# Weight conversion spread differently: one 64-bit chunk per attention turn instead of two, its scaling on GpSimd, and a new written order of a turn

## The chip, the cores and the metric

The kernel runs on 1 core of one Trainium2 chip. The metric is the device time of one execution in microseconds. "Before" was timed three times; the median is 724.79 us.

## The reference, cut to what matters

```python
def reference(**kw):                      # B=4, H=8, S=576, D=64, d_model=512, hidden 2048
    # attention with a learned relative bias
    scores = q @ k^T / 8 + bias(relu(x @ w1 + b1) @ w2)   # bias is [H, S, S], the same for all B
    attn = softmax(scores)                                # + 1e-9 in the divisor
    x = (attn @ v) as [B, S, 512]
    # Fourier mixing and a two-layer network
    u  = x + Re(fft(fft(x, axis=1), axis=2))
    un = (u - mean(u)) / sqrt(var(u) + 1e-6)
    return u + relu(un @ w_ch1) @ w_ch2
```

`w_ch1` (512 x 2048) and `w_ch2` (2048 x 512) arrive as 64-bit floats. Nothing on the chip multiplies 64-bit floats, so the kernel takes the two 32-bit words of each number and puts a 32-bit float together from them.

## The kernel before

**Stages.** First the bias of all eight heads is computed (up to about 62 us). Then come 16 units of attention, a unit being one pair of heads of one batch element. Unit n is worked on in "turn" n; a turn lasts about 13.6 us. After the last unit a tail mixes the first batch element, and from about 300 us the dense network runs: batch 0 alone (up to about 390 us), batch 1, batches 2 and 3 as a pair, and the 64 left-over rows of each.

**The turn.** `turn_of` (line 598) walks through a list of tokens, `ORDER`; TensorE, VectorE and ScalarE execute their shares in exactly that order, and so does SyncE, which issues the loads and stores. GpSimd's order is left to the compiler's scheduler. A quote after a token means "of the unit before", two quotes "two units before". The tokens are:

- `S0` to `S8`: TensorE computes one of nine score blocks into PSUM (line 276). Pool `sps` has two banks, so a block must wait for the `D` of the block two before it.
- `D0` to `D8`: VectorE adds the bias, writes the result to SBUF and takes the row maximum (line 297).
- `X0` to `X8`: ScalarE's exponential with row sums (line 312).
- `R'`, `P0'` to `P4'`: TensorE transposes the probabilities of the unit before into PSUM (line 444). `E''` transposes the finished output of the unit before that. They and the output `o` of the value product share two PSUM buffers (`place`), taken in turn, so that each waits until the one two before it has been read out.
- `VR0'`, `VR1'`, `V0'` to `V4'`: ScalarE copies a transposed tile to SBUF (line 434). With a small `v`, VectorE does it (line 436). In the order before, that one is tile 3.
- `A0'` to `A4'`: TensorE's value product, 40 matmuls (line 525). `O'`: ScalarE reads it out (line 536).
- `Q0'`, `Q1'`, `Y1''`, `Y2''`: the division by the row sum, on ScalarE and VectorE. Two tiny copies across the partition halves (line 550) go by DMA.
- `W0` to `W3` and `U0` to `U3`: the conversion (`widen`, line 154) of one chunk of `w_ch1` (`W`) and one of `w_ch2` (`U`), 128 x 512 numbers each: step 0 scales the upper word as a float on ScalarE (line 162), steps 1 to 3 are bit operations on VectorE (lines 167, 168, 169). After step 3 the chunk is stored as 32-bit floats in HBM and the next raw chunk is fetched.

In between, `prep` splits the next unit's q and k into a high and a low part on GpSimd (lines 215 and 219).

**Where the chunks go.** There are 16 of each weight. The turns listed in `WIDE`, twelve of the fifteen, convert one of each, so 24 of 32 are done in the attention. The turns 4 and 8 (and 1) convert none. The last turn (15) is written out in `TAIL`, which goes on with the mixing of batch 0. The other 8 are converted in dense batch 0 by `widen_rest`, there with all four steps on VectorE and with the raw loads issued by ScalarE. The list of these pieces is merged by weights with the layers and with the mixing of batch 1 (`run`); VectorE keeps the resulting order, the other engines' order is the scheduler's.

**A dense layer** (`layer`, `down`): ScalarE and GpSimd split the two weights into high and low parts (lines 1009, 1010), TensorE does 12 matmuls up (line 1044), ScalarE and VectorE make the two parts of the relu (`hh`, `hl`, lines 1052, 1053), TensorE does 12 matmuls down (line 1069), one layer later.

Of the kernel before, what the change touches and what calls it, by code (L numbers as in the profile page):

```python
# [20 lines left out]
P = 128  # L21
# [12 lines left out]
WIDE = [2, 3, 5, 6, 7, 9, 10, 11, 12, 13, 14, 15]  # L34
NEED = [0, 1, 3, 2]
KAT, QAT = 14, 36
# [13 lines left out]
S1 R' S2 VR0' X4' E'' D1 D2 Y1'' S0 VR1' Q0' D0 S4 Y2'' X1 P0' X2 S3 D4 V0' D3 P1' S6 Q1' D6 S7 V1' P2' V2' P3'  # L50
W0 D7 v3' X6 S5 S8 P4' D8 A0' D5 X0 V4' W1 A1' U0 A2' X8 X3 X5 W2 W3 U1 U2 A3' U3 X7 A4' O'
# [3 lines left out]
S1 S7' D1 D7' X7' S2 D2 P0' S4 V0' D4 P1' S8' S3 V1' D8' X8' X1 D3 P2' S6 V2' Q0' D6 P3' S0 R' Q1' D0 S7 V3'  # L55
VR0' vR1' P4' X0 D7 S8 V4' D8 S5 X2 D5 X3 A0' A1' A2' X8 X6 A3' X5 X7 A4' O'
# [74 lines left out]
def body(ctx, tc, a, out):  # L131
# [22 lines left out]
    def widen(src, dst, raw, q=nc.sync, on_act=True):  # L154
# [26 lines left out]
    vp = pool("vp", 3, stack=late, side="right")  # L181
# [238 lines left out]
    with ExitStack() as st:  # L420
# [99 lines left out]
        def value(u, j):  # L520
# [21 lines left out]
        def recip(u):  # L542
# [20 lines left out]
        def scaled(u, w):  # L563
# [22 lines left out]
            "Q": lambda u, w: (recip if w == "Q1" else add_tiny)(u),  # L586
# [11 lines left out]
        def turn_of(n, between):  # L598

            for i, w in enumerate(SECOND if n == 1 else ORDER):  # L600
                w, u = w.rstrip("'"), n - w.count("'")
                if w[0] in "WU":
                    if n in WIDE:
# [12 lines left out]
        orders = st.enter_context(ExitStack())  # L616
        wide, uf = {}, {}
# [4 lines left out]
        def fetch(which, n):  # L622

            if which == "W":
                f = rawp.tile([P, 512], F32, tag="wf", name="wf")
                t = widen(a["m1"][:, P * n:P * n + P].rearrange("(k p) c -> p k c", p=P), f, raw_tile(rawp))
                t.append(lambda: nc.sync.dma_start(w1_d[n].rearrange("p k c -> p (k c)"), f))
            else:
                f = rawu.tile([P, DM], F32, tag="wf", name="uf")
                t = widen(a["m2"][P * n:P * n + P], f, raw_tile(rawu))  # L630
                t.append(lambda: nc.sync.dma_start(w2_d[n], f))
                uf[n] = f
            wide[which] = t

        def widened(n, name):

            which = name[0]
            wide[which][int(name[1])]()
            if name[1] == "3":
                wide.pop(which)[4]()  # L640
                if n + 1 in WIDE:
                    fetch(which, WIDE.index(n + 1))

        for n in range(U - 1):
            pr = prep(n + 1) if n else []
            if n in WIDE and not wide:
                fetch("W", WIDE.index(n))
                fetch("U", WIDE.index(n))
            between = {3 + 6 * i: [piece] for i, piece in enumerate(pr)}
            if 2 <= n < U - 2:  # L650
                if n == 2:
                    orders.enter_context(tc.manual_schedule(engines={SP_}))
                for at, nm in ((KAT, "kT"), (QAT, "qT")):
                    between.setdefault(at, []).append(lambda nm=nm: load(n + 2, [nm]))
# [927 lines left out]
```

## Time and profile before

| what | value |
|---|---|
| median of three runs | 724.79 us (723.72 to 725.74) |
| the profiled execution's own time | 724.54 us |
| its span (first to last instruction) | 722.8 us |
| TensorE (PE) busy | 696.3 us, 96% of the span |
| VectorE (DVE) busy | 480.4 us, 66% |
| ScalarE (ACT) busy | 433.7 us, 60% |
| GpSimd (POOL) busy | 318.8 us, 44% |
| granted TensorE clock | 1.00 of full speed |

Busy time is the union of an engine's instructions. PE's matmuls overlap in the array, so a busy PE is not PE at its fastest; weight loads have a row of their own (PEld). Lines are those of the kernel printed above; "x40" means 40 instructions; "[0.37 <-DVE pt L436]" behind a row means that the engine sat idle for 0.37 us before it and that the write of `pt` by VectorE in line 436 ended the wait.

### The profile page before, as it was taken

Reading aid. Unit: us, or ns where it says so; the run is one execution under the profiler, and the core shown is the slowest. Engines: PE = TensorE matmul, PEld = TensorE weight load, DVE = VectorE, ACT = ScalarE, POOL = GpSimd, SP = SyncE. Lnnn points to the kernel's source line nnn. Section 1 sums busy time; section 2 is a strip of 40 time slices with the busy share of each in tenths; the row PEclk is TensorE's granted clock in tenths of the full one; section 3 lists DMA queues with packets and bytes.
Section 4 is the critical chain, followed back from the end, with each engine's and each line's share of the span. In section 5 each row is a group of like instructions: output and inputs, shape, how many; then the busy total and the mean of one; then the engine's idle time right before and its main releaser. Section 6 shows DMA issues by size and latency. Waiting matters only on the chain.

```text
span 722.8 us, 15194 instructions
## 1 busy us (share of the span) xinstructions
PE 696.3 (96%) x5735; PEld 557.7 (77%) x5735; DVE 480.4 (66%) x1010; ACT 433.7 (60%) x882; POOL 318.8 (44%) x274
## 2 busy tenths in 40 slices
PE   7898999999999999999999999999999999999997
PEld 4466777778778768788888888878788888888896
DVE  7997687997999977856663765566644334453443
ACT  7997998998999997433233443354433232344453
POOL 0002446446545552355644443568645442444342
PEclk9999999999999999999999999999999999999999
DMA  7878587598689663644321312113322224642432
GB/s 216 227 210 204 150 278 233 171 280 233 183 266 301 193 226 107 233 150 155 104 75 44 100 45 59 44 29 103 103 74 88 73 58 142 216 124 73 133 100 74
DMA packets 62521, 106.25 MB, mean 147 GB/s; under 512 B 8976, under 2 KB 28048, under 8 KB 61328
## 3 DMA queue, kind: packets, MB, share of 16 engines
q1 hardware_dynamic: 58720, 97.41, 45.2%
q10 hardware_dynamic: 3440, 4.78, 2.0%
q0 software_dynamic: 288, 3.08, 1.3%
q8 instruction: 45, 0.74, 0.4%
q14 instruction: 28, 0.23, 0.1%
HBM read 81.52 MB, written 21.07 MB: 142 GB/s over the span
## 4 chain that ended last, share of the span: by engine, by line
PE 72%; ACT 14%; DVE 6%; SPq 2%; issue 2%; DMA 2%; POOL 1%; ACTq 0%; DVEq 0%; POOLq 0%
PE hp L1044 15%; PE acc L1069 15%; PE acc L1319 12%; PE t L525 9%; ACT pt L434 5%; ACT p L312 5%; PE hpy L1288 3%; PE hpx L1288 3%; PE hpa L1288 3%; PE zp L745 3%; DVE pt L436 2%; PE abp L765 2%; SPq L345 2%; PE t L444 2%; PE hpb L1288 1%
## 5 line engine op out<-in xcount | busy, mean ns | idle before, releaser
L1010 POOL TENSOR_TENSOR w2l<-w2f,w2h 128x512 fp32r<-128x512 f32 x64 | 85.7, 1339 | 94.3 <-ACT w2h L1009 92.5
L297 DVE CUSTOM_DVE_ANT_0 p<-s,bias 128x576 f32<-128x576 f32 x128 | 93.0, 753 | 21.4 <-PE s L276 19.1
L1010 POOL TENSOR_TENSOR w1l<-w,w1h 128x512 fp32r<-128x512 f32 x55 | 72.2, 1314 | 70.6 <-ACT w1h L1009 68.3
L312 ACT ACTIVATE p<-p,nm 128x576 f32<-128x576 f32 x128 | 97.8, 766 | 0.8 <-DVE nm L297 0.8
L1009 ACT ACTIVATE w2h<-w2f 128x512 fp32r<-128x512 f32 x80 | 50.3, 629 | 56.9 <-PE acc L1069 22.6
L1053 DVE SCALAR_TENSOR_TENSOR hl<-hp,hh 128x512 fp32r<-128x512 f32 (+1 forms) x48 | 28.9, 601 | 78.9 <-ACT hh L1052 78.7
L525 PE MATMUL t<-pt,v 128*64 128x288 f32 x600 | 76.1, 409 | 3.3 <-DVE pt L436 3.3
L434 ACT ACTIVATE pt<-t 128x1024 f32<-128x1024 f32 (+2 forms) x113 | 72.9, 672 | 6.7 <-PE t L459 4.1
L1009 ACT ACTIVATE w1h<-w 128x512 fp32r<-128x512 f32 x55 | 34.7, 632 | 67.8 <-PE hp L1044 52.4
L525 PEld LDWEIGHTS t<-pt,v 128*64 128x64 f32 x600 | 41.7, 137 | 32.1 <-DVE pt L436 5.2
L1069 PE MATMUL acc<-w2h,hh 128*128 128x512 f32 x160 | 62.9, 394 | 0.0
L215 POOL TENSOR_SCALAR kh<-kT 128x640 fp32r<-128x640 f32 x14 | 11.0, 783 | 117.4 <-PE s L276 77.3
L1069 PE MATMUL acc<-w2l,hh 128*128 128x512 f32 x160 | 62.6, 392 | 0.0
L276 PE MATMUL s<-kh,qh 64*128 64x288 f32 (+1 forms) x320 | 58.5, 360 | 3.7 <-DVE nm L297 3.0
L1069 PE MATMUL acc<-w2h,hl 128*128 128x512 f32 x160 | 59.6, 392 | 0.0
L406 PE MATMUL bps<-hd,sm 128*32 128x288 f32 x432 | 51.1, 428 | 7.5 <-DVE hd L386 5.3
L444 PE MATMUL t<-ident,p 64*128 64x64 f32 x1080 | 46.9, 224 | 3.6 <-ACT pt L434 3.6
L1319 PE MATMUL acc<-w2h,hh 128*128 128x512 f32 x128 | 50.1, 391 | 0.0
L1319 PE MATMUL acc<-w2h,hl 128*128 128x512 f32 x128 | 49.9, 390 | 0.0
L1319 PE MATMUL acc<-w2l,hh 128*128 128x512 f32 x128 | 49.8, 389 | 0.0
L1044 PE MATMUL hp<-uh,w1h 128*128 128x512 f32 x124 | 49.1, 396 | 0.0
L1044 PE MATMUL hp<-uh,w1l 128*128 128x512 f32 x124 | 49.0, 395 | 0.0
(216 smaller groups left out, 1776.9 us busy)
## 6 DMA issues: line engine op xcount, KB each, us to landing
w2f<-w_d SPq DMA_DIRECT2D x80, 256.0 KB, 2.6
raw<-m SPq DMA_DIRECT2D x24, 512.0 KB, 5.4
w<-w_d SPq DMA_DIRECT2D x45, 256.0 KB, 3.2
qT<-qT SPq DMA_DIRECT2D x32, 288.0 KB, 4.6
bias_d<-ring SPq DMA_DIRECT2D x54, 144.0 KB, 2.7
bias<-bias_d SPq DMA_DIRECT2D x24, 288.0 KB, 5.5
kT<-kT SPq DMA_DIRECT2D x16, 320.0 KB, 5.3
v<-v SPq DMA_DIRECT2D x16, 320.0 KB, 6.0
```

The source lines that it names most:

```text
L276: nc.tensor.matmul(ps[:m, c, :CH], st[e, c0:c0 + m], mv[e, k0:k0 + CH], start=i == 0, stop=i == 2, skip_group_check=True)
L297: nc.vector.tensor_tensor_reduce(p, bank.pop((n, i))[:, :, :CH], bias, -0.125, 3.0e38, ALU.add, ALU.min, nms[n][:, blk:blk + 1])
L312: nc.scalar.activation(p, p, AF.Exp, bias=nms[n][:, blk:blk + 1], scale=-1.0, accum_out=sums[n][:, blk:blk + 1])
L434: nc.scalar.activation(dst, src, AF.Copy)
L444: nc.tensor.transpose(tp[:m, e, c0:c0 + 64], src[r], ident[r, r])
L525: nc.tensor.matmul(os_[u][e, c, :CH], vt[u][:, j, e], pts[u][:, 2 * j + h if j < 4 else 8, c * CH:(c + 1) * CH], start=j == 0, stop=j == 4 ...
L1009: nc.scalar.activation(h, src, AF.Copy)
L1010: eng.tensor_tensor(l, src, h.bitcast(F32), ALU.subtract)
L1044: nc.tensor.matmul(ps[:, :N], w[wi][:, P * kb:P * kb + P], ut[ui][:, kb, :N], start=i == 0, stop=i == len(mm) - 1)
L1069: nc.tensor.matmul(acc[t], h[i][:, P * t:P * t + P], w[j], start=f == 0 and k == 0, stop=f == NF - 1 and k == 2)
L1288: nc.tensor.matmul(self.ps[bank], w[wi][:, P * kb:P * kb + P], u[ui][:, kb], start=first and k == 0, stop=k == len(mm) - 1, skip_group_che ...
L1319: nc.tensor.matmul(self.acc[t], h[i][:, P * t:P * t + P], w[j], start=f == 0 and k == 0, stop=f == NF - 1 and k == 2)
```

## The change

Attention turn n (2 to 14) converts one chunk, named by `W`, and in turns 5 and 9 (`TWICE`) a second one, `U`. So 15 of the 32 are converted there and 17 in dense batch 0; the last turn converts none. Step 0 is done by GpSimd in the attention and by ScalarE in the dense batch, where the raw loads are now issued by SyncE. The stores and fetches have tokens of their own (`s`, `f`), as have the loads of q, k and v (`q`, `k`, `y`), the copies across the halves (`z'`), and GpSimd's pieces of `prep` (`K`, `L`, `M`), whose order is now kept on GpSimd too. `ORDER` itself is a new list: VectorE reads out tile 4 instead of tile 3, several exponentials are in other places, one (`X5'`) moved into the next turn. `SECOND` and `TAIL` are rewritten in the same way. Buffers: k's load tile shrinks and q's is doubled, the pool for v goes from 3 to 2.

```diff
-WIDE = [2, 3, 5, 6, 7, 9, 10, 11, 12, 13, 14, 15]
+TWICE = [5, 9]
+HALVES = 13 + len(TWICE)
+PREP = ["K1", "K2", "L1", "M1", "L2", "M2"]
...
 ORDER = """
-S1 R' S2 VR0' X4' E'' D1 D2 Y1'' S0 VR1' Q0' D0 S4 Y2'' X1 P0' X2 S3 D4 V0' D3 P1' S6 Q1' D6 S7 V1' P2' V2' P3'
-W0 D7 v3' X6 S5 S8 P4' D8 A0' D5 X0 V4' W1 A1' U0 A2' X8 X3 X5 W2 W3 U1 U2 A3' U3 X7 A4' O'
+U0 S1 U1 U2 D1 L1 R' VR1' VR0' X5' S2 M1 D2 Q0' E'' Y1'' S0 Y2'' D0 L2 P0' S4 V0' P1' V1' S3 D4 P3' q S6 P2' D3
+M2 V3' S7 D6 V2' S5 P4' X2 D7 S8 Q1' z' D8 X3 X4 X0 A0' D5 X8 X7 X6 A1' A2' v4' U3 K1 A3' K2 X1 k W0 W1 W2 A4' y
+O' W3 s f
 """.split()
...
 TAIL = """
-S1 R' S2 VR0' X4' E'' D1 D2 Y1'' p2 p5 S0 VR1' Q0' D0 S4 Y2'' X1 p0 P0' X2 S3 D4 V0' p1 p3 D3 P1' S6 Q1' p4 D6
-S7 V1' P2' V2' P3' W0 D7 v3' X6 S5 S8 P4' D8 A0' D5 X0 V4' g0 W1 A1' X8 g1 A2' X3 X5 h1 X4 h0 A3' X7 A4' O' -
...
+S1 R' D1 E'' S0 p0 X5' S4 VR1' VR0' p1 p3 Y1'' P0' X1 D0 V0' S2 D4 Y2'' D2 S6 X0 P3' V3' S3 p5 D6 P2' V2' S8 D3
+D8 P1' S7 P4' S5 V1' A0' Q0' Q1' z' D5 X6 D7 v4' A1' X4 A2' p4 X2 A3' g1 A4' p2 X8 g0 O' h1 - R0 B0 Z11 a11 h0
...
-    def widen(src, dst, raw, q=nc.sync, on_act=True):
+    def widen(src, dst, raw, q=nc.sync, on_act=False):
...
-            first = lambda: nc.vector.tensor_scalar(dst, hi.bitcast(F32), 2.0 ** -112, None, ALU.mult)
+            first = lambda: nc.gpsimd.tensor_scalar(dst, hi.bitcast(F32), 2.0 ** -112, 0.0, ALU.mult, ALU.add)
...
-            f = ldp.tile([P, 2 * S], F32, tag=nm, name=nm)
+            f = ldp.tile([P, 768 if nm == "kT" else 2 * S], F32, tag=nm, name=nm, bufs=1 if nm == "kT" else 2)
...
+                elif w in PREP:
+                    if pieces:
+                        pieces[PREP.index(w)]()
+                elif w in "kq":
+                    if 2 <= n < U - 2:
+                        load(n + 2, [w + "T"])
+                elif w == "y":
+                    if 1 <= n < U - 1:
+                        load_v(n + 1)
...
+            if n == 2:
+                ours.enter_context(tc.manual_schedule(engines={POOL_}))
+                orders.enter_context(tc.manual_schedule(engines={SP_}))
...
-                for f in range(1, len(WIDE)):
+                for f in range(1, (HALVES + 1) // 2):
                     w1_load(f)
                     if f < 3:
                         w2_load(f - 1)
+                    if f == 3:
+                        begin()
...
-                todo[k] = widen(src, dst, raws[k % 4], nc.scalar, False)
...
+            def start(h):
+                f = h // 2
+                raw = raws[h % 4]
+                if h % 2:
+                    dst = (rawp, rawd)[f % 2].tile([P, DM], F32, tag="wf", name="wf")
+                    todo[h] = widen(a["m2"][P * f:P * f + P], dst, raw, on_act=True)
+                    todo[h].append(lambda: nc.sync.dma_start(w2_d[f], dst))
+                else:
+                    dst = w1[f]
+                    todo[h] = widen(a["m1"][:, P * f:P * f + P].rearrange("(k p) c -> p k c", p=P), dst, raw, on_act=True)
...
+            for h in range(HALVES, 2 * NF):
+                early = .1 if h < HALVES + 2 else 1.
+                for c, i in ((.7, 0), (.7, 1), (.8, 2), (.9, 3)):
+                    res.append((c * early, lambda h=h, i=i: todo[h][i]()))
+                res.append((.05, lambda h=h: todo[h][4]()))
+                if h + 4 < 2 * NF:
+                    res.append((.05, lambda h=h: start(h + 4)))
...
-        run((main, 1.), (pcs, .94), (widen_rest(), .75))
+        run((main, 1.), (pcs, .94), (rest, .85))
```

## Rows read from the trace of the kernel before

**Rows 1.** Busy time by engine from one value product to the next, three turns.

```profile
core 0: us, PE busy (x) PEld busy (x) DVE busy (x) ACT busy (x) POOL busy (x), PEclk, DMA share, GB/s
116.11:129.67 13.56, 13.09 (x194) 10.21 (x194) 8.79 (x25) 11.93 (x28) 6.51 (x7) 1.00 0.64 183
157.53:171.10 13.57, 13.11 (x194) 10.20 (x194) 12.66 (x31) 13.07 (x31) 6.87 (x7) 1.00 0.91 273
171.10:184.68 13.58, 13.10 (x195) 10.19 (x195) 8.81 (x25) 11.95 (x28) 6.82 (x7) 1.00 0.65 182
```

**Rows 2.** The chain that ended last, through one turn: start, length, what.

```profile
211.81 5.07 PE t L525 x40
...
219.81 1.52 ACT p L312 x4
...
224.10 1.23 DVE pt L436
...
225.38 5.07 PE t L525 x40
```

**Rows 3.** Timeline of TensorE's weight loads in that turn, idle time in brackets.

```profile
216.81 0.19 PEld L276 LDWEIGHTS s<-kh,qh 64*128 64x128 f32 x2 [0.44 <-POOL kh L215]
...
217.19 0.40 PEld L444 LDWEIGHTS t<-ident,pr 64*128 64x128 f32 x8
...
218.38 0.19 PEld L276 LDWEIGHTS s<-kh,qh 64*128 64x128 f32 x2
...
220.75 0.65 PEld L444 LDWEIGHTS t<-ident,p 64*128 64x128 f32 x16
221.31 0.20 PEld L276 LDWEIGHTS s<-kh,qh 64*128 64x128 f32 x2
...
221.93 0.19 PEld L276 LDWEIGHTS s<-kh,qh 64*128 64x128 f32 x2 [0.17 <-DVE nm L297]
...
223.34 0.58 PEld L444 LDWEIGHTS t<-ident,p 64*128 64x128 f32 x16 [0.34 <-ACT pt L434]
```

**Rows 4.** Timeline of ScalarE and of VectorE in that turn.

```profile
221.35 2.86 ACT L434 ACTIVATE pt<-t 128x1024 f32<-128x1024 f32 x3
...
217.52 0.76 DVE L297 CUSTOM_DVE_ANT_0 p<-s,bias 128x576 f32<-128x576 f32 x1 [0.39 <-PE s L276]
...
220.44 0.74 DVE L297 CUSTOM_DVE_ANT_0 p<-s,bias 128x576 f32<-128x576 f32 x1
...
221.12 0.75 DVE L297 CUSTOM_DVE_ANT_0 p<-s,bias 128x576 f32<-128x576 f32 x1
```

**Rows 5.** Timeline after turn 5's value product: VectorE's second chunk, and GpSimd.

```profile
132.70 0.90 DVE L167 TENSOR_SCALAR raw<-raw 128x512 int32<-128x512 int32 x1
133.63 1.05 DVE L168 SCALAR_TENSOR_TENSOR raw<-raw 128x512 int32<-128x512 int32 x1
134.72 1.93 DVE L169 SCALAR_TENSOR_TENSOR uf<-uf,raw 128x512 int32<-128x512 int32 x1
...
134.10 2.00 POOL L219 TENSOR_TENSOR kl<-kT,kh 128x640 fp32r<-128x640 f32 x1
```

**Rows 6.** GpSimd by line and form, 80 to 266 us: busy, mean ns, idle before.

```profile
L215 POOL TENSOR_SCALAR qh<-qT 128x576 fp32r<-128x576 f32 x26 | 19.9, 784 | 34.8 <-DMA qT<-qT 34.8
...
L727 POOL TENSOR_TENSOR ge<-pq 128x512 f32<-128x512 f32 x2 | 2.6, 1281 | 0.2
```

**Rows 7.** Timeline of the last turn: ScalarE's queue, TensorE's weight loads.

```profile
262.74 1.16 ACTq L550 DMA_DIRECT2D rr<-rs  x2
...
265.02 0.58 PEld L444 LDWEIGHTS t<-ident,p 64*128 64x128 f32 x16 [1.32 <-ACT pt L434]
```

**Rows 8.** Dense batch 0: all engines, VectorE's conversion alone, its step 0 alone.

```profile
300.00:376.00 76.00, 76.00 (x359) 63.34 (x358) 49.36 (x88) 27.47 (x56) 40.63 (x32) 1.00 0.44 147
...
300.00:376.00 76.00, 25.23 (x32) 1.00 0.44 147
...
300.00:376.00 76.00, 4.56 (x8) 1.00 0.44 147
```

**Rows 9.** Waits from 299 to 400 us: total, times, longest.

```profile
DVE hl L1053 <- ACT hh L1052: 35.4, 13, 8.4
```

More of the change, by code (lines that the diff above doesn't have):

```diff
@@ L180, in body @@
     ldp = pool("ldp", 1, stack=late, side="right")
-    vp = pool("vp", 3, stack=late, side="right")
+    vp = pool("vp", 2, stack=late, side="right")
     sps = None
@@ L545, in recip, with across_halves @@
             nc.vector.reciprocal(rs, rs)
-            for h in range(2):
-                mine = slice(64 * h, 64 * h + 64)
-                other = slice(64 - 64 * h, 128 - 64 * h)
+            for h, mine in enumerate(half):
                 nc.vector.tensor_copy(rr[mine, h:h + 1], rs[mine, 8:9])
-                (nc.sync if u < U - 2 else nc.scalar).dma_start(rr[other, h:h + 1], rs[mine, 8:9])
+        def across_halves(u):
+            for h, mine in enumerate(half):
+                q = nc.sync if u < U - 2 else nc.scalar
+                q.dma_start(rrs[u][half[1 - h], h:h + 1], rss[u][mine, 8:9])
         def back(u, w):
@@ L615, in body @@
         fixed.enter_context(tc.manual_schedule(engines={PE_, DVE_, ACT_}))
-        orders = st.enter_context(ExitStack())
-        wide, uf = {}, {}
+        orders, ours = (st.enter_context(ExitStack()) for _ in range(2))
+        wide = {"next": 0, "held": 0, "now": 0}
         def raw_tile(rp):
             return rp.tile([P, DM], I64, tag="raw", name="raw")
[L622 to L627, printed above, removed]
-            else:
[L629 to L633, printed above, removed]
@@ L635, in widened, with fetch @@
-        def widened(n, name):
[L637 to L642, printed above, removed]
+        def fetch():
+            i = wide["next"]
+            f, wide["next"] = i // 2, i + 1
+            if i == HALVES:
+                return
+            rp = rawu if i % 2 else rawp
+            dst = rp.tile([P, DM], F32, tag="wf", name="wf")
+            if i % 2:
+                src, to = a["m2"][P * f:P * f + P], w2_d[f]
+            else:
+                src, to = a["m1"][:, P * f:P * f + P].rearrange("(k p) c -> p k c", p=P), w1_d[f].rearrange("p k c -> p (k c)")
+            wide[i] = widen(src, dst, raw_tile(rp)) + [lambda: nc.sync.dma_start(to, dst)]
@@ new lines, in widened @@
+        def widened(n, name):
+            if name == "f":
+                if units[n][1] == B - 1:
+                    wide["held"] += 1
+                else:
+                    fetch()
+                return
+            wide[wide["now"]][4 if name == "s" else int(name[1])]()
+            if name in ("s", "U3"):
+                if name == "U3":
+                    wide[wide["now"]][4]()
+                    fetch()
+                wide.pop(wide["now"])
+                wide["now"] += 1
@@ L644, in body @@
         for n in range(U - 1):
             pr = prep(n + 1) if n else []
[L646 to L654, printed above, removed]
@@ L655, in body @@
-            turn_of(n, between)
+            if n == 1:
+                for _ in range(2):
+                    fetch()
+            if n == 2:
+                ours.enter_context(tc.manual_schedule(engines={POOL_}))
+                orders.enter_context(tc.manual_schedule(engines={SP_}))
+            if wide["held"]:
+                wide["held"] = 0
+                fetch()
+            turn_of(n, pr)
             if n < 2:
                 load(n + 2)
-            if n == U - 3:
+            if n == U - 2:
@@ L1016, in rows_of, with dense @@
             return acc + [o[:, 0], o[:, 1]][:n // 2]
-        def dense(ut, tiles, store, n_first=0, mix=None):
+        def dense(ut, tiles, store, n_first=0, mix=None, begin=None):
             n = len(tiles)
@@ L1123, in step @@
-            def step(k, *which):
-                for i in which:
-                    if i < len(todo[k]):
-                        todo[k][i]()
-            def first():
-                for k in range(4):
-                    start(k)
-            res = [(.1, first), (1.5, lambda: None)]
-            for k in range(len(chunks)):
-                res += [(.7, lambda k=k: step(k, 0)), (.7, lambda k=k: step(k, 1)), (.8, lambda k=k: step(k, 2)),
-                        (.9, lambda k=k: (step(k - 1, 4) if k else None, step(k, 3)))]
-                if 0 < k < len(chunks) - 3:
-                    res.append((.05, lambda k=k: start(k + 3)))
@@ new lines, in first @@
+            def first():
+                for h in range(HALVES, HALVES + 4):
+                    start(h)
+            res = []
+            for h in range(HALVES, 2 * NF):
[5 more added lines that the diff above has]
+                    res.append((.05, lambda h=h: start(h + 4)))
@@ L1141, in run @@
+            return first, res
         def run(*streams):
@@ L1414, in body @@
         mix = Mix(1)
-        main, last_down, end = dense(ut, tl, row_store(0), 2, mix)
+        first, rest = widen_rest()
+        main, last_down, end = dense(ut, tl, row_store(0), 2, mix, first)
         tl, ut, pcs, fl = prepare([x[:, 1, t] for t in range(4)], mix)
-        run((main, 1.), (pcs, .94), (widen_rest(), .75))
+        run((main, 1.), (pcs, .94), (rest, .85))
         run((fl + last_down, 1.))
```

58 lines of the change are left out of this document (18 added, 40 removed).

## The prediction

> **What bounds the kernel now.** I read the busy times of the page first: PE is busy in 96% of the span. That cannot tell whether a shorter turn is possible, because overlapping matmuls count as busy while PE waits. So I looked for a comparison inside the kernel: windows cut from one value product to the next [rows 1]. The first and third cover turns 4 and 8, which convert nothing; the second is turn 7, which converts two chunks. VectorE has 8.8 us of work in the former and 12.66 in the latter, ScalarE 11.9 and 13.07, and all last 13.57 us. **So the two chunks cost the turn nothing.** Taking one out by itself will give nothing either; what counts is the order.
>
> Next the chain of waits through one turn [rows 2]. The value product holds PE from 211.81 to 216.81, 5.00 us, when the next scores begin [rows 2, 3]. From there to the next value product, at 225.38, are 8.57 us. The chain in them is ScalarE, not PE: the exponentials and the copies `V0'` to `V2'`, then `P3'`, which must wait until `V1'` has emptied its buffer (PE idle for 0.34 us), then VectorE's copy of tile 3, 1.23 us, until `A0'` may start.
>
> How much is PE's own work? Its loads are spaced by 0.38 us for a score block (216.81 to 217.19), 0.56 for a 16-transpose tile (220.75 to 221.31), and 1.19 for `R'`, `S2` and `E''` together (217.19 to 218.38) [rows 3]. Ten block shares (block `S0` has two) are 3.80, `R'` and `E''` 0.81, `P0'` to `P3'` 2.24, and `P4'`, half a tile, 0.28: 7.13 us. **So 1.44 us of each turn are PE waiting**; a perfect order would have turns of 12.13.
>
> **The change, part by part.**
>
> *The order of a turn.* I let the new list run by these rules, with t = 0 at `S1`: a block's `D` may start 0.71 after the block's first load (217.52 against 216.81); `D`s follow each other by 0.68, and a bank is free 0.81 after its `D` starts (221.12 to 221.93) [rows 3, 4]. A tile can be read out 0.76 after its first load (223.34 to 224.10) [rows 2, 3], and ScalarE needs 0.95 for one (2.86 for three) [rows 4].
>
> - PE: `S1` 0, `R'` 0.38, `S2` 0.75, `E''` 1.13, `S0` 1.57 (`D1` starts at 0.71, its bank is free at 1.52), `P0'` 2.35.
> - ScalarE: in the old turn `O'`, `VR0'`, `X`, `VR1'`, `Q0'` and two more `X` (1.52 [rows 2]) end where `V0'` begins, 4.54 after `S1` [rows 3, 4]. The new list has the same without those two: free at 3.02. `P0'` can be read at 3.11, so `V0'` runs from 3.1, `V1'` from 4.05, `V3'` from 5.0, `V2'` from 5.95 to 6.9.
> - PE goes on: `S4` 2.91, `P1'` 3.29, `S3` 3.87 (`D0` comes after `Y2''`, its bank is free at 3.81), `P3'` 4.25 (`V0'` over at 4.05), `S6` 4.81, `P2'` 5.19 (`V1'` over at 5.0), `S7` 5.75, `S5` 6.33 (`D6`; 0.2 late), `P4'` 6.71, `S8` 7.27 (`D7`; 0.27 late), end 7.66.
> - `A0'` needs `V2'`, over at 6.9. So it starts at **7.66**, not 8.57. The copy of tile 4 on VectorE is needed only by `A4'`, four microseconds later.
>
> The turn becomes 5.00 + 7.66 = 12.66. ScalarE fits: 6.9 plus eight `X` at 0.76 are 12.98, 0.3 after the value product, which `O'` takes out of its slack before `R'` is ready (1.1). Its work is 11.95 [rows 1] plus 0.95 for tile 3 less about 0.58 for tile 4, 12.3: nearly full. The list serves turns 2 to 14: 13 x 0.91 = **-11.8 us**. Bounds: 0.3 a turn if ScalarE and VectorE lose another 0.6 to waits (-4), 1.44 with no wait left (-18.7). I take the worked value, since the same rules give the old turn's starts back.
>
> *One chunk less, step 0 on GpSimd.* VectorE's work falls to 8.8 + 1.9 for three steps - 0.6 for the smaller tile, some 10.1 of 12.66. On GpSimd step 0 costs between 0.78, a scaling of 128 x 576, and 1.28, an operation of 128 x 512 with a reversed input [rows 6]; I take 0.9, as it reads every second word but has one input. GpSimd has 6.9 of work in a turn [rows 1], so 7.8. `W0` is queued behind `K2`, and `W1`, `W2`, `W3` and after them the next `D1` behind `W0`. By the list k is loaded right after `K2`, and `L1` may start when `S8` of the turn before is done, so `K2` should end some 3 us into the turn while `W1` is due at about 10: hidden. Cost 0, but see the third rival.
>
> *The load tokens.* They issue as many DMAs as before; the wait for `A4'` (`y`) and for `W3` (`s`) stands at the turn's end, and what is queued behind it is due a turn later. Cost 0; uncovered, a q or k load 5 us late would still come before its split. The two fetches and two more `U` in turns 5 and 9 lie in time that VectorE has. Cost 0.
>
> *The last turn.* There the ScalarE queue issues the two tiny copies (1.16 us) between `V0'` and `V1'`, and PE waits 1.32 instead of 0.34: 0.98 more [rows 7, 3]. The new list puts them behind `A0'`, but `X1` and `X0` (1.52) stand before `V1'`: 3.02 + 1.52 + 3.8 = 8.35, not 8.57 + 0.98. **-1.1 us**. Behind it VectorE loses two chunks' steps on the way to the norm, but PE has its own work there: -0.5 (0 to -2).
>
> *Dense batch 0.* Nine more chunks. Before, VectorE's conversion takes 25.23 us for 8 chunks, 4.56 of it step 0, which goes to ScalarE (27 of 76 us busy) [rows 8]. So 2.6 a chunk, and 17 take 44 instead of 25: VectorE goes from 49.4 to 68 of 76 us. It has the room on paper, but little: today it waits 35 us in all for `hh` [rows 9], which is slack that shrinks to some 15. PE needs `hl` only after the next layer's 12 matmuls, so short delays don't reach it. Bounds: 0 and, if the work piles up (all 44 us pushed into the first 0.85 with the mixing), 8 us. I take **+1**, nearer the lower, since 68 is below 76.
>
> **Sum**: -11.8 - 1.1 - 0.5 + 1.0 = -12.4 against the profiled execution's 724.54 (0.25 below the median): **712 us**.
>
> A rule that speaks against the change: the Trainium skill, page "SBUF — State Buffer", section "Who interferes with whom", says that a VectorE instruction with two SBUF inputs contends with a GpSimd instruction that reads SBUF, and that the second one to issue fully blocks until the first is done. The trace agrees: in turn 5 the three steps take 0.90, 1.05 and 1.93, 3.9 in all, while GpSimd splits k [rows 5]. This is the second rival.
>
> **The rivals.**
>
> 1. *The dense batch gives half back.* For: 68 of 76 us, VectorE's fixed order, and step 1 now has to wait for ScalarE's step 0 and a raw load queued on SyncE behind waiting weight loads. Against: the slack behind `hl`. Price: 6 instead of 1, 717 us.
> 2. *The chunk's steps are blocked in each turn.* GpSimd now also works while VectorE converts. With 3.9 instead of 1.9 us, behind `D8`, `D5` and the tile copy (over at 10.05), `W3` ends at 13.95, and `D1` is due at 12.66 + 0.71 = 13.37: 0.6 a turn, 7.8 in all, 720 us. For: turn 5. Against: most turns before don't show it (turn 7 has two chunks and no longer turn).
> 3. *GpSimd is late with step 0* (slower than before). VectorE would stand at `W1`, and so would `D1` and PE. It decides from the point where `K2` ends after about 11 us of a turn instead of 3, because k comes late: each us beyond that costs 13. At 2 us the turn is 12.66 + 2.0 = 14.66 and the time 712 + 26 = 738; 0.9 us late only cancels the gain. For: GpSimd waits for k and q in most turns already [rows 6]. Against: those waits are there because it is early.
> 4. *The new order moves the wait, it doesn't remove it* (ScalarE is 12.3 of 12.66 full, so every wait of it shows): turns stay at 13.4 or more, 723 us.
> 5. *Better than worked out*: the 0.5 us of late banks vanish as well, and the tail gives 2: 705 us.
>
> **How the numbers follow.** The forecast has 0.52, the rivals 0.14, 0.12, 0.08, 0.06 and 0.08. The likeliest case is 712, its own range 707 to 717. 0.3% of 724.79 is 2.2 us, about what this kernel's measurements can tell from no change. Faster: all of the forecast and of rivals 1, 2 and 5, 0.86, less 0.02 for their ends, with a little of 4: 0.84. Same: most of 4 and a bit of 3, 0.06. Slower: 0.10. Leaving out rival 3, rival 4 and the far ends gives the range 704 to 721.
>
> **What would show it.** Value products 12.5 to 12.9 us apart in turns 2 to 14; the chain through a turn running over PE's scores and transposes instead of ScalarE's copies and VectorE's tile copy; no PE wait of 0.34 before `P3'`; ScalarE over 95% busy; no VectorE wait for `W0`. In dense batch 0 VectorE about 68 of 76 us busy, and PE without a gap. The prediction is wrong if turns stay above 13.2, if VectorE waits for GpSimd in them, or if PE waits for `hl` or a weight in the dense batch.

## The result, and the profile after

The changed kernel takes **728.83 us** (median of five runs, 727.57 to 731.46) against 725.14 for the kernel before in the same session: ratio 1.0058, 95% interval 1.0031 to 1.0085. It is slower by 0.6%; 712, faster, was forecast. The profiled execution took 727.57 us, span 725.8 us.

The stages, read from the first weight load of each value product (a turn's length runs from the value product of the turn before to its own) and from VectorE's first addition at the end of dense batch 0 (us; the column "best" is the best kernel of the experiments):

| stage | before | after | best | forecast for the change |
|---|---|---|---|---|
| start to turn 1's value product | 75.40 | 76.00 | 74.66 | 0 |
| turns 2 to 14 | 177.11 | 174.33 | 167.55 | -11.8 |
| last turn | 14.55 | 13.75 | 13.72 | -1.1 |
| from there to the last value product | 20.89 | 20.99 | 21.01 | -0.5 |
| dense batch 0 | 108.98 | 116.62 | 111.36 | +1 |
| the rest | 325.8 | 324.1 | 323.8 | 0 |

So the turns gave 2.8 us of 11.8, and the dense batch took 7.6 instead of 1. (The 177.11 before holds one long turn, 6, of 14.30; the other twelve took 13.56 or 13.57.) Turns 2, 3, 7, 11, 13 and 14 last 12.9 us, near the forecast 12.66. Turns 4, 8 and 12, which load the bias of the next head pair, last 14.28, 14.12 and 13.72; turns 5 and 9, with a second chunk, 14.08 and 13.98, and the turns after these, 6 and 10, 13.30 and 13.56.

The busy windows of turns 3, 4 and 5, with the columns of [rows 1]; each ends at its turn's own value product, where the windows of [rows 1] begin:

```profile
88.88:101.77 12.89, 12.86 (x197) 10.19 (x195) 11.77 (x27) 12.49 (x28) 8.00 (x7) 1.00 0.62 182
101.77:116.05 14.28, 13.19 (x197) 10.26 (x195) 10.31 (x27) 12.63 (x28) 6.52 (x7) 1.00 1.04 289
116.05:130.13 14.08, 13.07 (x196) 10.24 (x194) 13.11 (x29) 12.48 (x28) 9.43 (x9) 1.00 0.57 168
```

In the long turns PE does the same work (13.1 to 13.2 us busy) and waits about 1 us more. The DMA share of turn 4 is 1.04: the engines are full. The chain of waits through turn 4 says for what (start, length, what):

```profile
103.31 0.55 SPq L552
...
103.90 6.98 DMA rr<-rs
...
110.98 0.30 DVE x L577
...
111.42 0.72 PE t L446 x16
```

`rr` is the handful of reciprocals that `Q1'` computes and `z'` sends to the other half of the partitions, for the product `Y2''` one turn later. The transfer needed 6.98 us in this turn. VectorE stood 1.38 us at `Y2''`. PE's transposes `P1'` go into the PSUM buffer that `Y2''` reads out, and began at 111.42, 0.14 us after its end. In turn 5 the chain goes another way:

```profile
120.37 1.67 DVE raw L169
...
122.06 0.85 DVE raw L170
...
123.02 0.74 DVE p L299
```

These are `U1` and `U2` of the second chunk, which the list puts ahead of `D1`. `U1` took 1.67 us; the median of step 1 in the turns is 0.56, the shortest 0.42. In that time GpSimd split q, and `U1` ended at 122.04, 0.3 us after this split:

```profile
119.99 1.75 POOL L221 TENSOR_TENSOR ql<-qT,qh 128x576 fp32r<-128x576 f32 x1
```

Dense batch 0: the window of [rows 8], and ScalarE's longest waits from 296 to 400 us (total, times, longest):

```profile
300.00:376.00 76.00, 70.42 (x331) 57.69 (x330) 58.74 (x84) 29.39 (x61) 35.30 (x28) 1.00 0.59 189
```

```profile
ACT w L164 <- DMA raw<-m: 19.9, 6, 6.7
ACT wf L164 <- DMA raw<-m: 18.5, 7, 5.5
```

PE has 70.4 us of work in 76 where it had 76.0. VectorE is not full (58.7; 68 was forecast); ScalarE stood 38 us at step 0, waiting for raw chunks. Its timeline and PE's weight loads show what stood behind one of these waits:

```profile
331.45 0.66 ACT L164 ACTIVATE wf<-raw 128x512 f32<-128x512 f32 x1 [1.66 <-DMA raw<-m]
332.01 0.62 ACT L1021 ACTIVATE w2h<-w2f 128x512 fp32r<-128x512 f32 x1
338.08 0.66 ACT L164 ACTIVATE w<-raw 128x512 f32<-128x512 f32 x1 [5.45 <-DMA raw<-m]
338.64 0.87 ACT L773 ACTIVATE z<-zp 128x256 fp32r<-128x256 f32 x4
```

```profile
339.83 0.77 PEld L781 LDWEIGHTS abp<-fd,z 128*128 128x128 f32 x6 [2.03 <-issue]
```

The copy of `z`, on which the mixing's next matmuls work, is queued behind the step 0 that waited 5.45 us; PE's 2.03 us gap ends after it.

### The profile page after: what moved, and what is told of

Same layout as the page of the kernel before. It is cut to its first block, busy times and chain, and to the rows that moved or that the text cites. A ratio compares the mean times of both kernels' runs of the same rounds, so it can differ in the third digit from the quotient of the medians.

```text
span 725.8 us, 15186 instructions
## 1 busy us (share of the span) xinstructions
PE 694.7 (96%) x5735; PEld 557.0 (77%) x5735; DVE 497.3 (69%) x1003; ACT 436.1 (60%) x874; POOL 333.7 (46%) x287
## 4 chain that ended last, share of the span: by engine, by line
PE 67%; DVE 12%; DMA 10%; ACT 4%; issue 3%; SPq 1%; POOL 1%; ACTq 0%; DVEq 0%; POOLq 0%
PE acc L1327 12%; PE acc L1081 10%; PE hp L1056 10%; PE s L278 8%; PE t L527 5%; PE t L446 4%; DMA raw<-m 4%; PE bps L408 4%; PE hpy L1296 3%; PE hpx L1296 3%; PE hpa L1296 3%; DMA rr<-rs 3%; DVE raw L170 3%; PE zp L761 2%; DVE raw L169 1%
## 5 line engine op out<-in xcount | busy, mean ns | idle before, releaser
L299 DVE CUSTOM_DVE_ANT_0 p<-s,bias 128x576 f32<-128x576 f32 x128 | 95.1, 756 | 26.9 <-PE s L278 23.0
L1022 POOL TENSOR_TENSOR w1l<-w,w1h 128x512 fp32r<-128x512 f32 x55 | 75.9, 1380 | 65.9 <-ACT w1h L1021 63.7
L436 ACT ACTIVATE pt<-t 128x1024 f32<-128x1024 f32 (+2 forms) x112 | 78.7, 732 | 13.3 <-PE t L446 7.2
L278 PE MATMUL s<-kh,qh 64*128 64x288 f32 (+1 forms) x320 | 60.9, 375 | 5.5 <-DVE nm L299 4.8
L1021 ACT ACTIVATE w1h<-w 128x512 fp32r<-128x512 f32 x55 | 34.6, 630 | 43.8 <-PE hp L1056 32.8
L217 POOL TENSOR_SCALAR qh<-qT 128x576 fp32r<-128x576 f32 x28 | 23.3, 833 | 56.3 <-DMA qT<-qT 47.7
L408 PEld LDWEIGHTS bps<-hd,sm 128*32 128x32 f32 x432 | 29.2, 116 | 25.6 <-DVE hd L388 6.3
```

Source lines behind the costliest of these rows:

```text
L278: nc.tensor.matmul(ps[:m, c, :CH], st[e, c0:c0 + m], mv[e, k0:k0 + CH], start=i == 0, stop=i == 2, skip_group_check=True)
L299: nc.vector.tensor_tensor_reduce(p, bank.pop((n, i))[:, :, :CH], bias, -0.125, 3.0e38, ALU.add, ALU.min, nms[n][:, blk:blk + 1])
L408: nc.tensor.matmul(ps[32 * t4:32 * t4 + 32, c, :CH], w2[:, int(rev)], h[:, c * CH:(c + 1) * CH], start=True, stop=True, tile_position=(0, ...
L436: nc.scalar.activation(dst, src, AF.Copy)
L1021: nc.scalar.activation(h, src, AF.Copy)
L1022: eng.tensor_tensor(l, src, h.bitcast(F32), ALU.subtract)
```

## The experiments

The stages below are from one profiled execution each; "dense" is from the last value product's start to VectorE's first addition. Two executions of kernels with the same dense batch differ by 0.1 to 0.7 us in it.

**Dense batch: who does step 0, and from which queue the raw chunks come.** The theory was that ScalarE's wait in step 0 costs; the rivals were the place of the loads on SyncE, and the number of chunks (a full VectorE).

```diff
-  todo[h] = widen(..., raw, on_act=True)
+  todo[h] = widen(..., raw, vec=True)                      # dense_step0_vector
+  todo[h] = widen(..., raw, nc.scalar, on_act=True)        # dense_loads_scalar_queue
+  todo[h] = widen(..., raw, nc.scalar, vec=True)           # dense_both_back
+  todo[h] = widen(..., raw)                                # dense_step0_gpsimd
```

`dense_step0_vector`. 

> In dense batch 0 step 0 of the 17 chunks is put on VectorE instead of ScalarE; the raw loads stay on SyncE, and the attention is that of the changed kernel. Theory 1, ScalarE blocked: the dense batch loses 7.6 us because ScalarE, which works in order, stands at step 0 until a raw load has landed (38 us of such waits), and the weight splits and relus queued behind it come late. Then most of the loss goes: from the value product of the last unit to the first output rows 110 to 112 us instead of 116.6, time 722 to 725. Theory 2, VectorE full: 17 chunks are too many for VectorE, wherever step 0 runs; another 17 x 0.57 us on it makes the stretch 118 us or more, time 730 or more.

Measured: 722.91 us, ratio 0.9972 (0.9932 to 1.0011); dense 112.81.

`dense_loads_scalar_queue`. 

> Only the queue of the raw loads in dense batch 0 is put back from SyncE to ScalarE; step 0 stays on ScalarE. Theory 1a, SyncE is late: the raw loads come late because they are queued on SyncE behind weight loads that wait for their buffers; then the loads start when their buffer is free, ScalarE's waits for them fall below 15 us and the time to about 724. Theory 1b, ScalarE asks too early: step 0 stands in ScalarE's order right where the load is expected to land, so that every load is waited for, whoever issues it; then waits and time stay, 727 to 730. Theory 2, VectorE full: no change, 728.

Measured: 727.7 us, 1.0036 (1.0006 to 1.0066); dense 115.78. ScalarE's waits for raw fell from 38.4 to 25.9 us and the stretch by 0.8 only.

`dense_both_back`. 

> Both parts put back in dense batch 0: step 0 on VectorE and the raw loads on ScalarE's queue, as in the kernel before, but for 17 chunks instead of 8. Theory 1: as with step 0 alone, 722 to 725, and a further gain only if SyncE's lateness matters. Theory 2, VectorE full: 730 or more, VectorE busy over 90% until the last chunk, TensorE waiting for hl.

Measured: 729.46 us, 1.0067 (1.0034 to 1.0099); dense 115.59, 2.8 more than with SyncE's loads.

`dense_step0_gpsimd`. 

> The changed kernel with step 0 of the chunks of the first dense batch on GpSimd (35 of 76 us busy there) instead of ScalarE, loads unchanged. Theory A (ScalarE's wait for raw chunks in its order blocks the relu parts behind it, worth 3.8 us): the dense stretch falls from 116.6 to 113 or less, as with step 0 on VectorE, and VectorE, with 8 to 10 us less to do than there, gains 0 to 2 us more: total 722 to 725. Rival B (GpSimd's own order holds the split of w1 behind the raw chunk in the same way): the dense stretch stays at 115 to 118, and PE waits for GpSimd's w1 parts; total 727 to 730.

Measured: 726.22 us, 1.0012 (0.9991 to 1.0034). The dense batch fell to 112.04, as theory A said. The total did not fall as far: the profiled execution, at 730.92 the slowest of ten (723.82 to 730.92), had turns 4, 5 and 12 of 16.5 to 16.8 us each.

The number of chunks, in the old code with its old way of converting (8 more in the dense batch):

```diff
-WIDE = [2, 3, 5, 6, 7, 9, 10, 11, 12, 13, 14, 15]
+WIDE = [2, 5, 7, 9, 11, 13, 14, 15]
```

`before_16_in_dense`. 

> The kernel before with only 8 of the 15 turns converting (two chunks each), so that 16 chunks instead of 8 are left to its dense batch 0, in its old manner (step 0 on VectorE, loads on ScalarE's queue). The turns should stay at 13.57 us, since turns without chunks are no shorter. Theory 1: the dense batch takes the additional 8 chunks at little cost, 725 to 727. Theory 2, VectorE full: it loses as much as the changed kernel's, 730 to 735.

Measured: 734.35 us, 1.0111 (1.0083 to 1.0138); ten turns stayed at 13.57, turns 10, 12 and 14 took 14.0 to 14.3, and dense took 117.21. And step 0 on ScalarE without one chunk more:

```diff
-  todo[k] = widen(src, dst, raws[k % 4], nc.scalar, False)
+  todo[k] = widen(src, dst, raws[k % 4], nc.scalar, True)
```

`before_step0_scalar`. 

> The kernel before with step 0 of the dense batch's 8 chunks on ScalarE instead of VectorE; loads stay on ScalarE's queue. Theory A (ScalarE stands at step 0 until a raw chunk has landed, and the copies and relu parts behind it with it, some 3 to 5 us whatever the number of chunks): dense stretch 111 to 113 instead of 109, ScalarE waits 10 us or more for raw, total 727 to 729.5. Rival B (the number of chunks is what costs, and VectorE gets 4.6 us free): dense stretch 107 to 109.5, total 723.5 to 726.

Measured: 730.66 us, 1.0075 (1.0052 to 1.0097); dense 114.35, that is 5.4 more with the same 8 chunks and 6.8 us less work on VectorE from 300 to 376 us. ScalarE's timeline at the head of that batch, and PE's loads:

```profile
298.33 0.68 ACT L162 ACTIVATE w<-raw 128x512 f32<-128x512 f32 x1 [2.21 <-PE hp L946]
299.18 0.67 ACT L162 ACTIVATE w<-raw 128x512 f32<-128x512 f32 x1 [0.16 <-DMA raw<-m]
300.77 0.66 ACT L162 ACTIVATE wf<-raw 128x512 f32<-128x512 f32 x1 [0.92 <-DMA raw<-m]
301.34 0.61 ACT L1009 ACTIVATE w1h<-w 128x512 fp32r<-128x512 f32 x1
```

```profile
302.00 0.19 PEld L1044 LDWEIGHTS hp<-uh,w1h 128*128 128x128 f32 x1 [3.21 <-ACT w1h L1009]
303.37 0.19 PEld L1044 LDWEIGHTS hp<-uh,w1l 128*128 128x128 f32 x1 [1.07 <-POOL w1l L1010]
```

Here the split of the weight, needed at once, stands behind three conversions whose chunks are only landing: 4.3 of the 5.4 us at one place, and behind it the granted clock was 0.50 from 304 to 306 us. So step 0 on ScalarE costs by itself. With 16 old-style chunks, or 17 with the loads on ScalarE's queue (117.21 and 115.59), the trace shows another wait: PE's longest are for VectorE's `hl` (3.68 us with 16; five of 0.8 to 1.5 us with 17), queued behind steps of the conversion, some of which took 1.5 to 1.7 us. So the second rival, VectorE, has a part there; what part was not measured.

**The late reciprocals.** One token pair of the new list goes back to where the old list had it, near `D4`:

```diff
-... V1' S3 D4 P3' q S6 P2' D3 M2 ... S8 Q1' z' D8 X3
+... V1' S3 D4 Q1' z' P3' q S6 P2' D3 M2 ... S8 D8 X3
```

`z_after_D4`. 

> The changed kernel with the other-half reciprocals (rr) computed and sent right after D4, as early as the old order had them, and nothing else moved. Theory A (turns 4, 8 and 12 are 1.2 us long each because the reciprocal copies are computed after S8 and their transfers stand in SyncE's list behind the bias, raw and query loads, so that Y2'' on VectorE waits for rr): those three turns fall from 14.28, 14.12, 13.72 to 12.9 to 13.1, the wait of VectorE for the transfer of rr is gone from them, total about 725 us (3 to 3.5 less than the changed kernel). Rival B (those turns are long because of the bias load's own stage, whatever the place of rr): less than 1 us is gained.

Measured: 720.88 us, 0.9945 (0.9927 to 0.9962). Turns 4, 8 and 12 are 12.91, 12.88 and 12.87, and VectorE never waits for `rr`. The 13 turns are 6.5 us shorter, not 3.5, because turns 5 and 9 are 12.9 too; `z_and_step0_vector` below shows that early reciprocals alone do not secure this second part. SyncE's list and VectorE's uses of `rr`, first after, then with the early reciprocals:

```profile
100.77 1.15 SPq L198 DMA_DIRECT2D qT<-qT  x2
102.02 1.20 SPq L245 DMA_DIRECT2D bias<-bias_d  x2
103.31 1.19 SPq L552 DMA_DIRECT2D rr<-rs  x2
```

```profile
110.98 0.29 DVE L577 TENSOR_TENSOR x<-t,rr 128x128 f32<-128x128 f32 x1 [1.38 <-DMA rr<-rs]
```

```profile
97.01 3.50 SPq L245 DMA_DIRECT2D bias<-bias_d  x4
100.60 1.19 SPq L552 DMA_DIRECT2D rr<-rs  x2
```

```profile
109.07 0.28 DVE L577 TENSOR_TENSOR x<-t,rr 128x128 f32<-128x128 f32 x1
```

Does lateness cost by itself? The same token moved in the old list, from `S6` to behind `S8`:

```diff
-... P1' S6 Q1' D6 S7 ... S5 S8 P4' D8
+... P1' S6 D6 S7 ... S5 S8 Q1' P4' D8
```

`before_rr_late`. 

> The kernel before with Q1' (the reciprocals and their transfers to the other half) moved from behind S6 to behind S8, and nothing else. Theory A (what is computed that late reaches the other half after Y2'' wants it in each turn that loads the bias): turns 4, 8 and 12 are longer by 1 us or more each, Y2'' waits for the transfer of rr, total 728 to 731. Rival B (only the new order, with its own place of the loads in SyncE's list and less time in a turn, makes the late reciprocals matter): turns stay at 13.57, total 725 to 726.

Measured: 726.63 us, 1.0014 (0.9992 to 1.0036): rival B. The transfer leaves at 103.33, as in the changed kernel, but `Y2''` wants it only at 111.28 instead of 109.60. It takes both, the late sending and the earlier use in the new turn.

**The second chunk.**

```diff
-TWICE = [5, 9]
+TWICE = []                                  # no_second_chunk
+TWICE = [3, 5, 7, 9, 11, 13]                # z_six_second_chunks, with the early reciprocals
+TWICE = [3, 5, 6, 7, 9, 10, 11, 13]         # z_eight_second_chunks, likewise
```

`no_second_chunk`. 

> The changed kernel with no turn converting a second chunk: 13 chunks in the turns, 19 in the first dense batch. Theory A (turns 5 and 9, and 6 and 10 after them, are long because U1 and U2 of the second chunk stand ahead of D1 on VectorE): the turns 5, 6, 9, 10 come to 12.9 to 13.0 and the attention stage is 3 to 3.4 us shorter; the dense batch takes 1 to 2 us more for two more chunks (about 0.85 to 1.0 us a chunk by the runs so far); total 726.5 to 727.5. Rival B (the conversion isn't what makes them long, contention for the GpSimd steps does or the loads): attention gains under 1 us and the total is 729.5 to 731.

Measured: 725.29 us, 0.9995 (0.9972 to 1.0017); dense 114.95. My theory A failed: turns 5 and 6 are 12.9, but turn 8 took 16.71 and turns 9 to 12 13.3 to 13.7, so the 13 turns took 175.75. The chain of waits through turn 8 is the reciprocals again:

```profile
149.85 6.82 DMA bias<-bias_d
...
156.69 6.83 DMA rr<-rs
...
163.61 0.30 DVE x L577
```

The turn is 3.8 us longer than 12.9, though PE stood only 2.23 us for this. The rest falls together with a lower TensorE clock: behind the wait PE is busy again, with a granted clock of 0.50, the lower level of 1.2 GHz (columns as in [rows 1]):

```profile
166.00:168.00 2.00, 2.00 (x28) 1.99 (x28) 0.92 (x4) 1.10 (x2) 1.92 (x3) 0.50 1.14 331
```

`z_six_second_chunks`. 

> Reciprocals sent after D4, and six turns (3, 5, 7, 9, 11, 13) convert a second chunk instead of two: 19 chunks in the turns, 13 in the dense batch. Theory A (the turns have time for them on VectorE, and the dense batch costs 0.85 us a chunk): all turns stay at 12.9, output at 278.1 to 278.5, dense stretch 112.5 to 113.5, total 717 to 718. Rival B (a second chunk delays D1): turns 3, 7, 11 and 13 come to 13.2 or more, and the total is 719 to 722. Rival C (the dense batch's cost hangs on how a chunk is converted there, not on how many are): turns as in A, dense stretch 116, total 720.5 to 721.5.

Measured: 721.26 us, 0.9943 (0.9920 to 0.9965); dense 111.64 with 13 chunks on ScalarE. In the profiled execution, at 726.16 the slowest of ten, turn 3 took 14.1 (`U1` 1.67 us beside a split) and turns 9, 10 and 11 took 14.8, 16.7 and 15.2.

`z_eight_second_chunks`. 

> As with six, but eight turns (3, 5, 6, 7, 9, 10, 11, 13) convert a second chunk: 21 in the turns, 11 in the dense batch. Theory A: turns 12.9, dense stretch 111 to 112, total 715.5 to 716.5. Rival B: second chunks in turns that follow each other (5, 6, 7 and 9, 10, 11) come late, because the loads of their raw chunks (512 KB each, some 6 us to landing) have one turn only; GpSimd waits for raw and with it VectorE's next D1, turns of 13.5 or more, total above 721. Rival C: dense stretch 116 whatever the number, total 720.5 to 721.5.

Measured: 749.02 us, 1.0323 (1.0282 to 1.0365): rival B. Turns 6, 7, 10 and 11 take 18.9 to 20.9 us. (Dense took 113.0 here with 11 chunks and 111.6 above with 13: no fixed price a chunk.) GpSimd's timeline, PE's loads, and windows of 2 us in turn 6 (columns as in [rows 1]):

```profile
128.27 0.66 POOL L166 TENSOR_SCALAR wf<-raw 128x512 f32<-128x512 f32 x1
137.43 0.64 POOL L166 TENSOR_SCALAR wf<-raw 128x512 f32<-128x512 f32 x1 [8.49 <-DMA raw<-m]
```

```profile
141.51 0.29 PEld L278 LDWEIGHTS s<-kh,qh 64*128 64x128 f32 x2 [5.95 <-DVE nm L299]
```

```profile
136.00:138.00 2.00, 0.00 (x0) 0.00 (x0) 0.00 (x0) 1.00 (x4) 0.57 (x1) 1.00 1.05 353
138.00:140.00 2.00, 0.00 (x0) 0.00 (x0) 1.87 (x2) 0.00 (x0) 1.92 (x3) 0.70 0.62 246
140.00:142.00 2.00, 0.49 (x4) 0.49 (x6) 2.00 (x4) 0.00 (x0) 1.92 (x3) 0.50 0.01 4
142.00:144.00 2.00, 2.00 (x30) 1.95 (x28) 1.57 (x5) 0.00 (x0) 1.92 (x3) 0.50 0.00 0
```

GpSimd stood 8.49 us for a raw chunk that SyncE could fetch only at 132.09, after `U3` of the turn before had freed its buffer; VectorE stood with `U1` and `D1` behind it, PE behind `D1`.

**The mends together.**

`three_mended` (early reciprocals, no second chunk, dense step 0 on VectorE). 

> The changed kernel with rr sent after D4, no second chunk in any turn (19 in the dense batch) and step 0 of the dense batch's chunks on VectorE. If the three costs add up: 3.5 and 3.4 us off the turns, 3.8 off the dense batch, 1 to 2.5 back for two more chunks there on a VectorE that is 70 of 76 us busy: 718.5 to 721 us, all attention turns from 2 on at 12.9. Rival (VectorE in the dense batch is full, and each chunk more is paid whole, with its steps of 0.6 to 1.1 us): the dense batch takes 115 us or more and the total is 721 to 724.

Measured: 719.25 us, 0.9924 (0.9902 to 0.9947); all turns 12.9, dense 115.32 with 19 chunks: the turns as forecast, the dense batch as the rival.

`z_and_step0_vector` (early reciprocals, dense step 0 on VectorE). 

> Reciprocals sent after D4, second chunks kept in turns 5 and 9 (17 chunks in the dense batch), step 0 of the dense batch on VectorE. Theory A (the dense batch loses 3.8 us to step 0 on ScalarE, whatever the turns do): attention as with the early reciprocals alone (output at 278.1), dense stretch 112.5 to 113.5 instead of 116.4, total 716.5 to 718. Rival B (the dense stretch differs between executions by more than that, and step 0's engine makes nothing): dense stretch 115 to 117, total 719.5 to 721.5.

Measured: 718.07 us, 0.9886 (0.9870 to 0.9903); dense 112.94. Here turns 5 and 9 were 14.08 and 13.68 again, with `U1` at 1.66 us in turn 5 and `U2` at 1.77 in turn 9: the second chunk can cost also with early reciprocals, where its steps fall together with a split on GpSimd.

`z_and_step0_gpsimd` (early reciprocals, dense step 0 on GpSimd). 

> Reciprocals sent after D4, step 0 of the dense batch's 17 chunks on GpSimd. Theory A (112.0 us of the dense stretch in the run with GpSimd's step 0 alone came from an emptier ScalarE and VectorE): dense stretch 112 to 113, total 716 to 717.5, the best so far. Rival B (that stretch was short only because the attention had ended late, so that loads stood ready): 115 to 117 and 719.5 to 721.

Measured: **715.12 us, 0.9849 (0.9830 to 0.9868)**, the best. All turns 12.9, dense 111.36. Its turns 4 and 5, its dense window, and GpSimd's waits for raw there:

```profile
100.44:113.33 12.89, 12.89 (x196) 10.19 (x194) 10.11 (x27) 12.48 (x28) 5.68 (x6) 1.00 0.98 307
113.33:126.21 12.88, 12.88 (x196) 10.19 (x195) 11.81 (x29) 12.48 (x28) 9.77 (x10) 1.00 0.55 158
300.00:376.00 76.00, 74.18 (x349) 61.59 (x347) 70.89 (x98) 26.18 (x53) 54.27 (x45) 1.00 0.57 187
```

```profile
POOL wf L166 <- DMA raw<-m: 8.1, 5, 4.0
POOL w L166 <- DMA raw<-m: 4.8, 3, 3.6
```

GpSimd waits 12.9 us for raw where ScalarE waited 38, and PE has 74.2 of 76 us.

`best_no_second_chunk` (the best one with `TWICE = []`). 

> Early reciprocals, dense step 0 on GpSimd, and no second chunk in any turn (19 in the dense batch). Theory A (the second chunk of turns 5 and 9 is free here, and two more chunks in the dense batch cost 0.3 us each): all turns 12.9, output at 277 to 278, dense stretch 112, total 715 to 716.5. Rival B (the second chunks do cost in most executions): the median falls to 713 to 714.5.

Measured: 717.81 us, 0.9884 (0.9851 to 0.9917); all turns 12.9, dense 111.77 with 19 chunks in the profiled execution, the fastest of four (714.84 to 719.30). Taking the second chunks out gains nothing there.

`best_no_vector_steps` (VectorE's steps left out of the dense batch). 

> Early reciprocals, dense step 0 on GpSimd; steps 1 to 3 on VectorE are left out for the 17 chunks of the dense batch (so the weights used there are only the high words scaled), loads, step 0 and stores stay. This prices VectorE's 36 us of conversion there. Theory A (with step 0 away from ScalarE VectorE's share is nearly hidden): dense stretch 108 to 111, 0.5 to 3 us less than the 111.4 with them, total 712 to 714.5. Rival B (VectorE at 71 of 76 us is still what bounds the dense batch): 106 or less, total below 710.

Measured: 714.16 us, 0.9832 (0.9802 to 0.9861). Dense 108.72 with PE busy 76.00 of 76, as before the change. VectorE's 17 conversions thus cost 2.6 us once step 0 is off ScalarE. The profiled execution is the slowest of four, 717.5 us; its turn 9 took 16.53, and this is the chain of waits into it:

```profile
154.73 6.42 DMA qT<-qT
...
166.44 1.56 POOL kl L221
168.00 0.67 POOL wf L166
...
171.69 1.66 DVE raw L169
```

The load of q landed late, GpSimd's splits with it, `W0` behind the last of them, and `U1` then fell beside the next split.

## Why the prediction was wrong, point by point

- **What bounds a turn: right.** The score-to-value stretch was ScalarE's chain, and the new list removes it. In the best kernel's turn 4 the chain of waits holds PE alone, where [rows 2] alternated with ScalarE and VectorE:

```profile
100.52 5.00 PE t L527 x40
...
111.43 1.09 PE s L278 x12
112.52 0.24 PE t L446 x8
112.76 0.64 PE s L278 x5
```

- **The size of the turn: 12.89, not 12.66.** The worked starts hold to `S8` (7.29 against 7.27); `A0'` comes 0.23 later, so the step from the last score block to the value product is 0.6, not 0.39. That is 3.0 us of the 11.8 over 13 turns, and 13 turns of 12.89 against 13.57 are worth 8.8.
- **The step that failed: the order as a whole was costed by PE's and ScalarE's starts, and the move of `Q1' z'` behind `S8` was not costed at all.** I replayed the engines and left SyncE's list out; the part on the load tokens priced the loads, stores and fetches at 0 and passed over `z'`. `rr` is then computed 2.8 us later (0.5 instead of 3.3 us ahead of the turn's value product), is sent behind q and bias loads, and takes 6.4 to 7.4 us to land in turns 4 and 8, where the bias is loaded. With the pair put back the 13 turns are 6.5 us shorter than in the changed kernel: 3.45 in turns 4, 8 and 12, the rest the second chunks' share. Three other kernels that kept it late lost 5.3, 8.2 and 15.0 in their profiled executions, against the same turns with the pair early. The fourth rival had the price (the wait is moved, turns of 13.4 or more; the mean is 13.41), but for a full ScalarE, which was not what happened.
- **"Two more U in turns 5 and 9: cost 0" holds only where GpSimd is not splitting just then.** Beside a split `U1` takes 1.66 us instead of 0.43, ahead of `D1`, and turn 5 is 1.2 us longer, in the changed kernel and in `z_and_step0_vector`; in `z_after_D4` and in the best kernel, where `U1` ran before the split, it cost nothing. The kernel before had shown the price: its turn 6, which [rows 5] open, lasted 14.30 instead of 13.57, and the prediction read these rows for the second rival alone. That rival's mechanism is thus real, at another place: the single chunk's steps, at the turn's end, were lengthened too (`W3` up to 1.8 us) without a longer turn.
- The rule of the Trainium skill (page "SBUF — State Buffer", section "Who interferes with whom") was drawn on for instructions with two inputs; `U1` has one. The same section adds that `tensor_scalar` can enter modes that use both port pairs, and then contends. The trace agrees: 1.66 us beside the split, 0.42 to 0.43 where none ran.
- **Third rival: not in the changed kernel's turns, but real.** Step 0 on GpSimd took 0.65 to 0.71 us there (0.9 was taken), and VectorE never waited for it. In `best_no_vector_steps` it came late by the rival's own way, behind `K2` after a late load (turn 9, 16.53). With second chunks in neighbouring turns GpSimd was late because of the raw chunk, and the time went to 749.
- **Dense batch 0, the other step that failed: +7.6 instead of +1.** I sized VectorE's load (44 us for the 17 chunks, measured 43.8; 68 of 76 in all, 70.9 in the best kernel) and gave ScalarE step 0 free of charge because it had 27 of 76 us of work. Busy time was the wrong measure. ScalarE works in order, and a step 0 that waits for a raw chunk holds up weight splits, relu parts and mixing copies. Moving step 0 alone to VectorE gave back 3.4 to 3.8 us, to GpSimd 4.6 to 5.0; what is left, 2.4, is VectorE's share (2.6 by the run without its steps), where 1 was taken. The first rival named this wait with the price 6, and put it on VectorE's step 1. The length of the waits is not the price: with the loads on ScalarE's queue they fell by 12.5 us and the batch by 0.8, and in `z_six_second_chunks`, with 13 chunks, ScalarE still waited 26.6 us for raw while the batch took 111.64. That it counts what stands behind a wait is shown at single places only, and no kernel with 13 chunks had step 0 elsewhere, so what step 0 costs there stays open.
- **The last turn** gave 0.8 of 1.1 (the starts worked out, 8.35 against 9.55, say 1.2): the two copies are issued at 264.40, behind the start of the value product at 264.08; **the tail behind it** nothing (+0.1 for -0.5).
- **Not forecast:** the rest of the program is shorter in all kernels with the new code (323.6 to 324.5, against 325.6 to 326.3 with the old), in the changed kernel by 1.7 us. I did not follow this up.

Two of the signs of being wrong that the prediction gave came: turns above 13.2 on the mean, and in the dense batch PE waits for a weight (`w1l`, 1.3 us) and for `hl` (1.4 us). With both faults mended the time is 715.12, inside the range (704 to 721): -9.6 in the turns, -0.8 in the last, +2.4 in the dense batch. Part of that is luck: 0.7 of the 9.6 is the long turn 6 of the kernel before, and the 2.7 us by which the start and the rest of the program are shorter were in no sum.

## What to carry to other kernels

When an order is rewritten, replay the queue that issues transfers together with the engines: for each small transfer whose send has moved, find what it now stands behind, its time to landing in the busiest turn, and the moment of its use in the new, shorter turn. Before giving an engine work that waits for a load, ask what else stands in its order behind that work; its idle share says nothing about this. Put such work on the engine whose queue can best afford to stand.

## What the runs showed of the hardware beyond this

- A transfer of 64 values (`rr`) lands after 1.6 to 7.4 us (median 3.7) in the changed kernel; the 6.98 us on the chain of turn 4 fall where the bias is loaded and the DMA share is 1.04.
- A wait on PE can cost more than its length. In the changed kernel PE stood up to 1.26 us in turns 4 to 12, the granted clock stayed 1.00, and the turns grew by 0.4 to 1.4 us. In the turns of 16.5 to 16.8 us in other kernels PE stood 2.1 to 2.4 us, its clock then fell to 0.50 to 0.58 in windows of 2 us, and the turns grew by 3.6 to 4.0 us. Not after each such wait: in turn 11 of `z_six_second_chunks` PE stood 2.27 us, the clock stayed 1.00, and the turn grew by 2.3 us. In the kernel with eight second chunks PE stood for 5.95 us; its granted clock was then 0.70 and 0.50 (the lower level, 1.2 GHz) in the windows from 138 to 142 us, and still 0.50 from 142 to 144 us, with PE busy again: the turn grew by 7.8 us.
